# A new order table for a fused RWKV-5 attention and squared-ReLU MLP: engine orders, PSUM banks and filling matmuls

## The chip, the cores and the metric

The kernel runs on one core of a Trainium2 chip. A core has five engines, each of which works off its own queue of instructions in order: TensorE (PE) multiplies matrices into PSUM (eight banks of 128 x 512 float32), VectorE (DVE) and ScalarE (ACT) do elementwise work, GpSimd (POOL) and SyncE (SP) here mainly issue DMAs. The metric is device time in microseconds, median of several executions.

## The reference

Inputs are r, k and v of 4 batches x 8 heads x 768 positions x 48, w and u of 8 x 48, and the MLP's weights of 384 x 2048 and 2048 x 384, all float32.

```python
def _attn_ref(r, k, v, w, u):
    B, H, S, D = r.shape                       # 4, 8, 768, 48
    state = np.zeros((B, H, D, D), dtype=np.float32)
    y = np.zeros_like(r)
    for t in range(S):
        kt, vt, rt = (k[:, :, t].copy(), v[:, :, t].copy(), r[:, :, t].copy())
        cur = np.einsum('bhd,bhe->bhde', u[None] * kt, vt)
        y[:, :, t] = np.einsum('bhd,bhde->bhe', rt, state + cur)
        state = w[None, :, :, None] * state + np.einsum('bhd,bhe->bhde', kt, vt)
    return y

def _moe_ref(x, w_in, w_out):
    h = x @ w_in
    r = np.maximum(h, 0.0)
    g = r * r
    return g @ w_out

# x = attn_out.transpose(0, 2, 1, 3).reshape(3072, 384); out = _moe_ref(x, w_in, w_out)
```

## The kernel before

The 768 positions are cut into six chunks of 128. A unit is one chunk of one batch, so there are 24, numbered chunk by chunk: units 0 to 3 are the first chunk of the four batches. For each unit the attention is computed with matrices of 128 x 128 (positions by positions) for what lies within the chunk, and with a state of 48 x 48 per head for what came before; then the unit's 128 rows go through the MLP.

One unit runs through these steps; the token that stands for each in the table is in brackets, with the engine and the line.

- Load r, k and v (`rt`, `kt` by SP, `vt` by POOL, line 311, or `vtS` by SP, line 309). For units 0 to 5, r and k come in two halves of four heads each (`rt.3.1` is the second half of unit 3's r, line 281) two of them issued by ACT and the others by SP. From unit 6 on (`NH = 6`) one DMA loads two units (line 278).
- Scale r and k by powers of w (`scale.i.0` for r, `scale.i.1` for k; DVE, line 303 for units 0 to 5, line 301 later), into a bf16 tile named rkw. Then both are transposed: in units 0 to 5 by PE (`turn`, line 333) with a copy out of PSUM by ACT (`rkT`, line 337), from unit 6 on by a transposing DMA of SP for two units (`rkD`, line 322).
- For units 0 to 5, k is turned back for the state (`kb`, PE, line 345; `kbT`, ACT, line 349). The product r·k is formed (`rk`, DVE, line 360 or 357).
- Positions by positions (`at`, PE, line 369), masked to the strict lower half on the way out of PSUM (`mask`, DVE, line 377, two halves).
- The diagonal's sums and the state's product (`d` and `s`, PE, lines 389, 398 and 410), the diagonal times v (`dv`, DVE, line 420), the state's update (`sadd`, `sdec`, DVE, lines 424 and 428; bf16 copy `stb`, ACT, line 432). v is cast to bf16 by ACT (`vb`).
- y (`y`, PE, lines 441 and 447), and its copy with dv added (`yb`, DVE, line 456), then its transpose, by PE and ACT (`xturn`, `xT`, lines 477 and 481) or by SP's DMA for two units (`xD`, line 467).
- First matmul of the MLP (`m1.i.q`, PE, line 493: four quarters of one unit, or eight eighths for two units together), `relu` (ACT, line 501), the square (`sqA` on ACT, line 508, or `sqD` on DVE, line 510), second matmul (`m2.i.q`, PE, line 517; the last unit in two halves, line 533), copy out (`osb`, ACT, line 524; lines 543 and 545 for the last unit) and store (`out`, SP, line 553 or 549).

Besides these there are steps that run once: powers of w on ACT and DVE, `ids` and `upper` (POOL builds identities and the mask), `cols`, `copied` and `uwb` (w and u as columns, by PE, DVE and POOL), `end` (ACT: the 128th power of w) and `wend` (POOL, line 268: spread over the state's blocks; it reads what `end` writes), and the weight loads, `I.0` to `I.3` (POOL, line 288, a quarter of the first weight matrix each) and `O.0` to `O.3` (POOL, line 291, of the second). `fill.n` is n matmuls on a constant tile (line 216) whose result nothing reads.

What stands in which order on each engine is written out: `ORDER`, a table of tokens in lines 16 to 80, is walked once from its start to its end, and each token issues its step at the end of its engine's queue. So an engine's order is the order in the table of the tokens that run on it, and the table's relative order between engines has no effect but on the synchronization of buffers. `@` behind a token names the PSUM bank or banks of its output. SP's and POOL's DMAs go into two different queues. The loads of r, k and v rotate through four buffers of two units each.

```python
    for word in ORDER.split():
        what, _, where = word.partition("@")
        name, *a = what.split(".")
        ...
        if where:
            place.update(zip(names(name, *a), (int(x) for x in where)))
        steps[name](*a)
```

Of the kernel before, what the change touches and what calls it, by code (L numbers as in the profile page):

```python
# [16 lines left out]
kt.0.0 kt.0.1 rt.0.0 rt.1.0 I.0 rt.1.1 vt.0 ktA.1.0 lnat.0 fill.26 log@4567 kt.1.1 lnat.1 ids rt.2.0 w.1 upper w.0  # L17
fill.8 cols@1 rt.2.1 wk scale.0.0 kt.2.0 zeros scale.0.1 wr fill.8 turn.0.0@2 kt.2.1 copied uwb turn.0.1@5 rkT.0.0
rt.3.0 rkT.0.1 vt.1 rk.0 fill.10 at.0@63 scale.1.0 rt.3.1 I.3 kb.0@4 mask.0.0 d.0@2 turn.1.0@7 I.2 kbT.0 kt.3.0
mask.0.1 rkT.1.0 vt.2 scale.1.1 vb.0 I.1 kt.3.1 fill.19 turn.1.1@4 dv.0 y.0@3 rkT.1.1 rt.4.0 yb.0 vb.1 rk.1 fill.9  # L20
kb.1@4 kt.4.0 scale.2.0 at.1@31 xturn.0@6 rt.4.1 mask.1.1 d.1@5 turn.2.0@2 xT.0 rkT.2.0 scale.2.1 kt.4.1 fill.5
# [5 lines left out]
kbT.3 m1.2.0@6 scale.4.1 relu.1.1 dv.3 m1.2.1@4 rkT.4.0 sqD.1.3 sqA.0.2 y.3@7 m1.2.2@1 scale.5.0 relu.2.1 sqD.1.1
m1.2.3@2 relu.2.2 sqD.0.1 s.3@5 sqA.1.2 turn.4.1@4 m2.0.0@3 sadd.3 relu.2.3 sadd.2 m2.1.0@1 rkT.4.1 yb.3 relu.2.0
m2.1.1 rk.4 vb.4 scale.5.1 kb.4@7 stb.1 xturn.3@6 at.4@42 kbT.4 m2.0.1 mask.4.1 xT.3 stb.0 s.4@5 mask.4.0 turn.5.0@6
m1.3.0@2 sqD.2.1 rkT.5.0 y.4@0 dv.4 relu.3.0 turn.5.1@6 rt.8 sadd.4 m1.3.3@7 rkT.5.1 yb.4 m2.1.2 sqA.3.0 sqA.2.0  # L30
m2.0.2 kt.8 xturn.4@2 m2.0.3 xT.4 scale.6.0 kb.5@5 osb.0 m2.1.3 scale.7.0 relu.3.3 m1.3.1@2 vtS.6 kbT.5 vb.5
m1.4.0@6 scale.6.1 scale.7.1 at.5@75 relu.4.0 m2.2.0@0 mask.5.0 osb.1 rkD.6 sqA.4.0 m1.4.1@4 sqD.2.3 sqA.2.2 sqD.3.3
m1.4.2@1 relu.3.1 mask.5.1 m2.2.1 stb.3 sdec.4 m1.4.3@6 relu.4.2 rt.10 rk.5 y.5@5 sqA.4.2 scale.8.0 s.5@2 scale.8.1
relu.4.1 m2.2.2 scale.9.0 relu.4.3 vtS.8 m1.3.2@1 sqD.3.1 stb.4 m2.3.0@4 dv.5 relu.3.2 yb.5 m2.2.3 scale.9.1 kt.10
m2.3.1 osb.2 sadd.5 sqA.4.1 m2.4.0@1 sqD.4.3 vb.6 xturn.5@0 sdec.5 at.6@2376 xT.5 rk.6 rkD.8 m2.4.1 stb.2 mask.7.0
stb.5 m1.5.0@0 sqA.3.2 mask.6.0 s.7@7 relu.5.0 mask.7.1 m1.5.3@5 mask.6.1 s.6@2 relu.5.3 m2.4.2 dv.6 out.0 vb.8
y.6@3 dv.7 rt.12 y.7@0 yb.6 m1.5.1@6 yb.7 m2.3.2 sadd.6 relu.5.1 xD.6 scale.10.0 m2.4.3 sqA.5.0 scale.10.1 sqA.5.1
m2.3.3 sadd.7 vtS.10 osb.4 m1.5.2@6 scale.11.1 scale.11.0 m2.5.0@3 relu.5.2 sqD.5.3 kt.12 m2.5.1 sqA.5.2 rk.8
at.8@1520 osb.3 sdec.6 m2.5.2 mask.9.0 rkD.10 m2.5.3 mask.8.0 s.8@4 mask.8.1 osb.5 s.9@2 m1.6.0@7 mask.9.1 m1.6.1@6
sadd.8 relu.6.0 dv.9 kt.14 m1.6.3@5 relu.6.1 dv.8 m1.6.7@1 sqA.6.0 scale.12.0 sadd.9 sqA.6.1 y.9@3 rt.14 y.8@4 vb.10  # L40
m1.6.2@0 yb.8 stb.6 m1.6.5@2 yb.9 relu.6.3 sdec.9 xD.8 m1.6.4@6 relu.6.5 scale.12.1 m2.7.0@3 relu.6.2 sqD.6.3
relu.6.7 vtS.12 m2.6.0@4 scale.13.0 relu.6.4 scale.13.1 m1.6.6@7 sqA.6.2 rk.10 at.10@6120 sqA.6.4 rkD.12 m2.6.1
relu.6.6 mask.10.0 sqA.6.5 s.10@5 sdec.7 m2.7.1 sqA.6.6 sqD.6.7 m2.7.2 stb.7 mask.10.1 stb.9 out.1 m2.7.3 sadd.10
kt.16 mask.11.0 y.10@6 osb.7 m1.8.0@1 dv.10 m1.8.1@2 rt.16 scale.14.0 relu.8.0 sdec.8 m1.8.3@5 relu.8.1 mask.11.1
m2.6.2 stb.8 yb.10 sqA.8.1 s.11@3 y.11@2 relu.8.3 dv.11 m1.8.6@1 vb.12 yb.11 m1.8.4@6 relu.8.6 sadd.11 xD.10 m2.6.3
rk.12 sqA.8.0 relu.8.4 scale.15.0 m1.8.2@2 scale.14.1 m1.8.5@0 relu.8.2 sdec.10 out.4 m2.9.0@7 osb.6 scale.15.1
vtS.14 sqA.8.2 sqD.8.3 m2.8.0@6 relu.8.5 out.3 at.12@4312 sqA.8.6 rkD.14 s.12@0 sqA.8.5 mask.13.0 m2.8.1 sqA.8.4
mask.12.1 m1.8.7@5 mask.12.0 m1.10.1@1 relu.8.7 mask.13.1 out.2 m1.10.3@3 relu.10.1 scale.16.0 vtS.16 s.13@4 sadd.12
y.12@2 dv.12 rt.18 m2.8.2 sdec.11 m1.10.6@5 yb.12 m1.10.5@0 dv.13 relu.10.6 sqD.8.7 y.13@2 stb.10 m2.9.1 relu.10.5
scale.17.0 yb.13 sqA.10.6 m2.8.3 sadd.13 relu.10.3 xD.12 m1.10.2@0 osb.8 sqD.10.3 sqA.10.1 m1.10.0@3 scale.16.1  # L50
kt.18 m1.10.7@1 relu.10.0 scale.17.1 rt.20 at.14@5642 relu.10.2 rk.14 sqA.10.0 m2.9.2 mask.15.1 vb.14 m2.9.3
# [571 lines left out]
```

## Time and profile before

| | us |
|---|---|
| median of 3 runs | 170.97 |
| lowest, highest | 170.62, 171.13 |
| the profiled execution's own time | 171.94 |
| its span | 170.2 |

In the profiled execution the mean granted TensorE clock is 0.988 of full speed. 28.86 MB are moved by DMA, 148 GB/s of reads and writes of device memory over the span. Matmuls of line 493 are 720 with 251 ns each, of line 517 368 with 326 ns each.

How to read the profile: busy time is the time in which an engine executed an instruction, and PEld is the loading of weights into PE, beside its matmuls. In a group's row, `out<-in` names the tiles, `xN` the count, and the bracket behind it the idle time just before the group and what ended it (`<-`). In the chain of waits, and in a list by time, the first two numbers of a row are the start and the length in us. In the DMA queues' rows, the queue's name is followed by packets, megabytes and the time its packets took as a share of all 16 DMA engines. A row with `SPq` or `POOLq` in the list of issues ends with the size and the time from issue to landing. Half a clock of PE is a granted clock of 0.50 in the table by stage.

### The profile page before, as it was taken

What the parts mean: (1) busy time and instruction counts of PE and PEld (TensorE: products, weight loads), DVE (VectorE), ACT (ScalarE), POOL (GpSimd) and SP (SyncE); (2) the same over time, 40 slices, a digit from 0 to 9 for tenths busy, and PEclk for the clock granted to TensorE, in tenths of its full rate; (3) what the DMA queues carried; (4) which work ended last, traced back from release to release, by engine and by line L of the source; (5) the groups of instructions that cost most, each with busy time, mean ns of one, the idle gap of its engine ahead of it and who ended that gap; (6) DMA issues with size and microseconds to landing.
All of it is one profiled execution on the core that took longest, in us unless ns stands there. A gap on an engine that the chain in (4) does not pass through costs nothing.

```text
span 170.2 us, 4733 instructions
## 1 busy us (share of the span) xinstructions
PE 163.9 (96%) x1947; PEld 134.1 (79%) x1947; DVE 122.3 (72%) x243; ACT 129.8 (76%) x255; POOL 15.7 (9%) x36
## 2 busy tenths in 40 slices
PE   7959999999999999999999999999999999999993
PEld 7649999778787697886977887787889789688672
DVE  6567999876999989988988888989697662101100
ACT  3735999888796489698499679688699739599921
POOL 7770670000000000000000000000000000000000
PEclk9996999999999999999999999999999999999999
DMA  3999999999999899999999997998990501100044
GB/s 92 172 279 240 272 194 254 213 201 227 185 181 218 153 214 190 181 212 191 236 182 202 174 251 173 188 288 197 180 232 4 179 6 54 42 0 4 0 164 162
DMA packets 91493, 28.86 MB, mean 170 GB/s; under 512 B 82864, under 2 KB 90672, under 8 KB 91472
## 3 DMA queue, kind: packets, MB, share of 16 engines
q1 hardware_dynamic: 88416, 23.99, 67.5%
q0 software_dynamic: 2624, 4.33, 12.9%
q8 instruction: 15, 0.25, 0.6%
q10 hardware_dynamic: 432, 0.25, 0.6%
q14 instruction: 6, 0.05, 0.1%
HBM read 20.50 MB, written 4.72 MB: 148 GB/s over the span
## 4 chain that ended last, share of the span: by engine, by line
PE 87%; DMA 6%; DVE 3%; SPq 2%; issue 1%; DVEq 0%
PE bank L493 36%; PE bank L517 34%; DMA rt<-in_r_dram 4%; PE bank L369 4%; PE bank L441 3%; DMA xT<-yb 2%; PE bank L398 2%; PE bank L447 2%; SPq L281 2%; PE bank L533 2%; PE bank L333 1%; PE bank L410 1%; PE bank L345 1%; PE bank L216 1%; PE bank L477 1%
## 5 line engine op out<-in xcount | busy, mean ns | idle before, releaser
L493 PE MATMUL bank<-xT,w_in_q 128*128 128x256 bf16 (+1 forms) x720 | 72.6, 251 | 0.1
L501 ACT ACTIVATE gr<-bank 128x512 f32<-128x512 f32 x96 | 55.3, 604 | 19.0 <-PE bank L493 15.2
L517 PE MATMUL bank<-w_out_q,g 128*128 128x384 bf16 x368 | 68.6, 326 | 0.0
L493 PEld LDWEIGHTS <-w_in_q 128*128 128x128 bf16 x720 | 63.8, 113 | 3.9 <-DMA xT<-yb 0.3
L517 PEld LDWEIGHTS <-g 128*128 128x128 bf16 x368 | 34.3, 98 | 18.1 <-issue 0.2
L508 ACT ACTIVATE g<-gr 128x512 bf16<-128x512 f32 x68 | 41.2, 636 | 0.2
L377 DVE TENSOR_TENSOR am<-bank,smask 128x512 bf16<-128x512 f32 x48 | 31.3, 684 | 7.4 <-PE bank L369 6.6
L510 DVE TENSOR_TENSOR g<-gr 128x512 bf16<-128x512 f32 x28 | 19.0, 686 | 17.2 <-ACT gr L501 17.2
L524 ACT COPY osb<-bank 128x384 f32<-128x384 f32 x23 | 11.0, 480 | 5.7 <-PE bank L517 5.6
L456 DVE TENSOR_TENSOR yb<-bank,dv 128x384 bf16<-128x384 f32 x24 | 12.9, 553 | 3.2 <-PE bank L447 2.3
L420 DVE TENSOR_TENSOR dv<-vb,bank 128x384 f32<-128x384 bf16 x24 | 13.0, 548 | 2.2 <-PE bank L410 1.4
L432 ACT CAST stb<-st 128x384 bf16<-128x384 f32 x20 | 10.2, 522 | 0.6 <-DVE st L428 0.6
L301 DVE TENSOR_TENSOR rkw<-rt,wpos 128x384 bf16<-128x384 f32 x18 | 9.8, 551 | 0.8 <-DMA rt<-in_r_dram 0.7
L301 DVE TENSOR_TENSOR rkw<-kt,wneg 128x384 bf16<-128x384 f32 x18 | 9.7, 551 | 0.8 <-DMA kt<-in_k_dram 0.8
L337 ACT COPY rkT<-bank 128x512 bf16<-128x512 bf16 x12 | 7.0, 590 | 3.4 <-PE bank L333 3.4
L216 PE MATMUL bank<-warm 128*128 128x128 bf16 x87 | 8.4, 265 | 1.1 <-DVE warm L161 1.1
L441 PE MATMUL bank<-vb,am 128*128 128x48 bf16 x192 | 8.9, 185 | 0.0
L428 DVE TENSOR_TENSOR st<-st,wend 128x384 f32<-128x384 f32 x16 | 8.8, 550 | 0.0
L424 DVE TENSOR_TENSOR st<-bank,st 128x384 f32<-128x384 f32 x16 | 8.7, 549 | 0.0
L441 PEld LDWEIGHTS <-am 128*128 128x128 bf16 x192 | 7.9, 97 | 0.8
L369 PE MATMUL bank<-rkT 64*128 64x128 bf16 x192 | 8.2, 221 | 0.2 <-ACT rkT L337 0.2
L216 PEld LDWEIGHTS <-warm 128*128 128x128 bf16 x87 | 7.0, 121 | 1.2 <-DVE warm L161 1.0
(75 smaller groups left out, 120.8 us busy)
## 6 DMA issues: line engine op xcount, KB each, us to landing
out_dram<-osb SPq DMA_DIRECT2D x23, 192.0 KB, 2.4
rt<-in_r_dram SPq DMA_DIRECT2D x9, 384.0 KB, 5.8
kt<-in_k_dram SPq DMA_DIRECT2D x9, 384.0 KB, 5.2
vt<-in_v_dram SPq DMA_DIRECT2D x9, 384.0 KB, 4.5
w_in_q<-in_moe_w_in_dram POOLq DMA_DIRECT2D x4, 384.0 KB, 8.3
w_out_q<-in_moe_w_out_dram POOLq DMA_DIRECT2D x4, 384.0 KB, 8.8
vt<-in_v_dram POOLq DMA_DIRECT2D x6, 192.0 KB, 7.3
kt<-in_k_dram SPq DMA_DIRECT2D x11, 96.0 KB, 5.2
```

Source lines behind the costliest of these rows:

```text
L216: nc.tensor.matmul(out=banks[0][:, :128], lhsT=warm, rhs=warm, start=True, stop=True)
L301: nc.vector.tensor_tensor(t["rkw"][:, x, :, :, :D], pair(src), pair(wneg if x else wpos), ALU.mult)
L369: nc.tensor.matmul(out=t["at"][o][:, p, :], lhsT=t["rkT"][sl, 1, p, :], rhs=t["rkT"][sl, 0, p, :], start=True, stop=True,)
L377: nc.vector.tensor_tensor(am, t["at"][o], smask.unsqueeze(1).to_broadcast([C, HP, C]), ALU.mult)
L420: nc.vector.tensor_tensor(t["dv"], t["vb"], t["d"].unsqueeze(2).to_broadcast([C, H, D]), ALU.mult)
L441: nc.tensor.matmul(out=y[:, 2 * p + o, :], lhsT=t[f"am{o}"][:, p, :], rhs=t["vb"][:, 2 * p + o, :], start=(o == 0 and p == 0), stop=c == 0 ...
L456: nc.vector.tensor_tensor(t["yb"], t["y"], t["dv"].rearrange("p h d -> p (h d)"), ALU.add)
L493: nc.tensor.matmul(out=t["h", s][:, a], lhsT=turned, rhs=chunks[c]["xT"][:, b : b + m, n, :], start=(n == 0), stop=(n == NK - 1),)
L501: nc.scalar.activation(t["gr", s], t["h", s], AF.Relu)
L508: nc.scalar.activation(g, x, AF.Square)
L510: nc.vector.tensor_tensor(g, x, x, ALU.mult)
L517: nc.tensor.matmul(out=t["o"], lhsT=chunks[units[i][0]]["g"][:, f, units[i][1], :], rhs=w_out_q[f // 4][:, f % 4, :], start=(f == 0), stop ...
```

## The change

The table of tokens is replaced by another one. Both tables hold the same steps with the same engines; the functions are untouched. Three things differ: the order of the tokens, the bank numbers behind `@`, and the filling matmuls (eight groups of 26, 8, 8, 10, 19, 9, 5 and 2 = 87 before; 26, 20, 10, 9, 3, 13, 1 and 9 = 91 now). Nearly every line of the table is another one; two lines of each, both with `wend`, stand here for them:

```diff
 ORDER = """
...
-scale.3.0 relu.0.3 wend xturn.1@7 rk.2 at.2@26 xT.1 kb.2@0 mask.2.1 sqA.0.0 kt.5.0 d.2@4 turn.3.0@3 vt.3 s.0@7
...
+d.0@1 mask.0.1 end vb.0 kt.3.1 wend scale.1.1 rkT.1.0 fill.13 y.0@3 rt.4.0 dv.0 vt.2 fill.1 turn.1.1@4 yb.0 rt.4.1
...
```

Three places in detail. The first is SP's queue in the opening. Its rows are the loads of halves of r and k; the tiles kt_227 (now kt_217) and rt_206 belong to units 2 and 3, rt_351 and kt_370 (now rt_354 and kt_372) to units 4 and 5. Before:

```order
L281 DMA kt_227<-in_k_dram 128x1x192 x2
L281 DMA rt_206<-in_r_dram 128x1x192 x2
L281 DMA kt_227<-in_k_dram 128x1x192 x2
L281 DMA rt_351<-in_r_dram 128x1x192
L281 DMA kt_370<-in_k_dram 128x1x192
L281 DMA rt_351<-in_r_dram 128x1x192
L281 DMA kt_370<-in_k_dram 128x1x192
```

Now:

```order
L281 DMA kt_217<-in_k_dram 128x1x192 x3
L281 DMA rt_206<-in_r_dram 128x1x192 x2
L281 DMA kt_217<-in_k_dram 128x1x192
L281 DMA rt_354<-in_r_dram 128x1x192 x2
L281 DMA kt_372<-in_k_dram 128x1x192 x2
```

The first half of unit 3's k, which stood behind both halves of its r, now stands ahead of them; and the halves of unit 4 come as r, r, k, k where they alternated.

The second place is POOL's queue in the opening and, behind it, DVE's steps of units 4 and 5. On POOL, vt are loads of v, w_in_q and w_out_q quarters of the two weight matrices, and wend is the copy that waits for ACT's `end`. Before:

```order
L311 DMA vt_162<-in_v_dram 128x8x48
L288 DMA w_in_q3_150<-in_moe_w_in_dram 128x3x512
L288 DMA w_in_q2_149<-in_moe_w_in_dram 128x3x512
L311 DMA vt_310<-in_v_dram 128x8x48
L288 DMA w_in_q1_148<-in_moe_w_in_dram 128x3x512
L268 COPY wend_146<-wend_c_145 64x4x48 x2
L311 DMA vt_310<-in_v_dram 128x8x48
L291 DMA w_out_q0_151<-in_moe_w_out_dram 128x1536
```

Now:

```order
L311 DMA vt_203<-in_v_dram 128x8x48
L288 DMA w_in_q3_150<-in_moe_w_in_dram 128x3x512
L268 COPY wend_146<-wend_c_145 64x4x48 x2
L311 DMA vt_358<-in_v_dram 128x8x48
L288 DMA w_in_q2_149<-in_moe_w_in_dram 128x3x512
L288 DMA w_in_q1_148<-in_moe_w_in_dram 128x3x512
L291 DMA w_out_q0_151<-in_moe_w_out_dram 128x1536
```

`wend` moved ahead of two quarters of the first weight matrix and one load of v, and `O.0`, the first quarter of the second weight matrix, now follows the last quarter of the first one directly. On ACT, `end` moved from unit 1's part of the table to unit 0's.

On DVE, rkw_129 holds scaled r and k of units 4 and 5, am are masks, g squares, st states. From unit 5's scaled r on, before:

```order
L303 TENSOR_TENSOR rkw_129<-rt,wfour 128x8x48
L510 TENSOR_TENSOR g<-gr 128x4x128 x2
L424 TENSOR_TENSOR st_3_140<-bank_256,wend 128x384
L424 TENSOR_TENSOR st_2_139<-bank_76,wend 128x384
L456 TENSOR_TENSOR yb<-bank_258,dv 128x384
L360 TENSOR_TENSOR rk<-rkT 128x512
L303 TENSOR_TENSOR rkw_129<-kt,wfour 128x8x48
L377 TENSOR_TENSOR am_787<-bank_78,smask 128x512
L377 TENSOR_TENSOR am_799<-bank_255,smask 128x512
```

Now:

```order
L303 TENSOR_TENSOR rkw_129<-rt,wfour 128x8x48
L360 TENSOR_TENSOR rk<-rkT 128x512
L510 TENSOR_TENSOR g<-gr 128x4x128 x2
L303 TENSOR_TENSOR rkw_129<-kt,wfour 128x8x48
L377 TENSOR_TENSOR am_784<-bank_76,smask 128x512
L377 TENSOR_TENSOR am_791<-bank_78,smask 128x512
```

Unit 5's scaled k stands ahead of unit 4's masks in both; two updates of the state and a yb that stood between unit 5's r and k stand elsewhere now.

The third place is SP's queue in the middle, from the transposing DMA of units 14 and 15 (rkw3) to that of units 16 and 17 (rkw0). Its other rows are loads of pairs, a transpose of y (xT) and stores. Before:

```order
L322 DMA_TRANSPOSE rkT_1667<-rkw3_130 128x16x128
L553 DMA out_0_dram<-osb_1066 128x384
L309 DMA vt_1715<-in_v_dram 128x16x48
L278 DMA rt_1740<-in_r_dram 128x16x48
L467 DMA_TRANSPOSE xT_1795<-yb_1753 128x6x128
L278 DMA kt_1814<-in_k_dram 128x16x48
L278 DMA rt_1825<-in_r_dram 128x16x48
L322 DMA_TRANSPOSE rkT_1862<-rkw0_127 128x16x128
```

Now:

```order
L322 DMA_TRANSPOSE rkT_1650<-rkw3_130 128x16x128
L553 DMA out_0_dram<-osb_1260 128x384
L309 DMA vt_1712<-in_v_dram 128x16x48
L278 DMA kt_1749<-in_k_dram 128x16x48
L467 DMA_TRANSPOSE xT_1805<-yb_1758 128x6x128
L278 DMA rt_1822<-in_r_dram 128x16x48
L278 DMA rt_1833<-in_r_dram 128x16x48
L553 DMA out_0_dram<-osb_1831 128x384
L278 DMA kt_1878<-in_k_dram 128x16x48
L553 DMA out_0_dram<-osb_1322 128x384
L322 DMA_TRANSPOSE rkT_1912<-rkw0_127 128x16x128
```

One more load and two more stores stand between the two transposes now.

More of the change, by code (lines that the diff above doesn't have):

```diff
@@ L16 @@
 ORDER = """
[L17 to L21, printed above, removed]
@@ L27 @@
[L27 to L31, printed above, removed]
@@ L32 @@
[L32 to L51, printed above, removed]
@@ new lines @@
+turn.5.0@6 sqA.1.2 m2.0.0@1 scale.5.1 stb.0 s.3@7 relu.2.2 mask.4.0 m2.0.1 xT.3 mask.4.1 m2.1.1 vb.4 rkT.5.0 m2.1.2
+s.4@0 y.4@3 dv.4 rt.8 turn.5.1@6 m1.3.0@5 sadd.3 rkT.5.1 yb.4 m2.0.2 relu.3.0 sadd.4 kb.5@6 m2.0.3 sdec.4 vtS.6
+m1.3.3@5 scale.6.0 osb.0 sqA.2.0 scale.7.0 xturn.4@2 m1.3.2@3 kbT.5 kt.8 xT.4 m2.1.3 vb.5 scale.6.1 m1.3.1@6 osb.1
+scale.7.1 stb.3 m2.2.0@0 rk.5 sqA.3.0 rkD.6 sqD.2.1 at.5@74 relu.3.3 m1.4.0@1 mask.5.1 relu.3.1 s.5@5 mask.5.0
+sqA.2.2 m1.4.2@2 relu.4.0 sqD.2.3 m1.4.3@6 stb.1 sqD.3.3 relu.4.2 kt.10 m2.2.1 sadd.5 relu.3.2 m1.4.1@1 sqD.3.1
@@ L80 @@
+m2.23.1@5 osb.22 out.22 osb.23.1 out.23.1
 """
```

88 lines of the change are left out of this document (56 added, 32 removed).

## The prediction, made before the changed kernel was run

> **What bounds the kernel now.** I read the page's busy times first, then a table by stage, then who waits for whom, and last the DMA queues. In the table the columns are the stretch, its length, and for PE, PEld, DVE, ACT and POOL the busy time with its count; then the granted clock, the mean share of the DMA engines and GB/s.
>
> ```profile
> PE 163.9 (96%) x1947; PEld 134.1 (79%) x1947; DVE 122.3 (72%) x243; ACT 129.8 (76%) x255; POOL 15.7 (9%) x36
> ...
> 8.90:12.30 3.40, 1.46 (x23) 1.29 (x23) 2.17 (x5) 1.43 (x3) 2.85 (x4) 1.00 1.11 285
> 12.40:15.80 3.40, 3.40 (x42) 3.01 (x43) 2.27 (x5) 1.07 (x3) 0.00 (x0) 0.50 1.17 218
> 15.82:31.00 15.18, 15.18 (x269) 13.85 (x268) 14.90 (x30) 15.10 (x34) 5.82 (x9) 1.00 1.08 240
> ...
> 60.00:126.00 66.00, 65.94 (x749) 53.63 (x747) 58.24 (x111) 54.26 (x104) 0.00 (x0) 1.00 1.08 206
> ```
>
> From 15.82 us on PE is busy without a gap at full clock; the order cannot shorten that work, since both tables hold the same steps. A new order can gain only ahead of it, and lose anywhere. Two more things are full. DVE and ACT are busy 14.90 and 15.10 us of the 15.18 up to 31 us, and the DMA engines stand at a share of about 1 from 9 to 126 us. So the question for each moved step is which load or DVE step now arrives last.
>
> The opening, in order of time:
>
> ```profile
> 10.13 0.56 DVE L303 TENSOR_TENSOR rkw<-rt,wfour 128x384 bf16<-128x384 f32 x1 [1.63 <-DMA rt<-in_r_dram]
> 10.74 0.40 PE L333 MATMUL bank<-identb,rkw 128*128 128x128 bf16 x4 [1.84 <-DVE rkw L303]
> 12.40 0.61 PE bank L333 x4
> 13.33 0.96 PE bank L216 x9
> 14.29 0.43 PE bank L345 x4
> 14.72 0.54 PE bank L369 x8
> 15.26 0.43 PE bank L477 x3
> 15.78 0.31 PE bank L333 x4
> 16.37 0.66 PE bank L493 x11
> ```
>
> DVE waits 1.63 us for unit 1's r, PE 1.84 us for DVE; then PE works at half clock to 15.8, and m1.0.0 starts at 16.37 (all rows with "PE bank" are from the chain).
>
> **The change, part by part.** *Opening.* Up to turn.1.1 (12.40) the same loads decide, and they stand in the same order. copied now stands ahead of scale.0.1 on DVE, turn.0.1 uses turn.0.0's bank, and there are four more fills (91 for 87): all of it lies ahead of the 10.74 row, under the 1.63 us wait, and I cost it at nothing; without that cover it would be up to the spacing of one DVE step, 0.5 us. Behind 12.40 PE has, ahead of m1.0.0, turn.1.1, nine fills, xturn.0, kb.1, at.1 and turn.2.0: by the rows above 0.61 + 0.96 + 0.43 + 0.43 + 0.54 + 0.31 = 3.28 us, so m1.0.0 at 15.7 where it was at 16.37 (y.0 is done earlier; d.1 and seven fills move behind it or go). That is 0.7 us ahead at half clock, up to twice that if the clock isn't halved. But turn.3.0 stands 2.8 us of PE work later and needs both halves of unit 3's r:
>
> ```profile
> 10.05 0.54 SPq L281 DMA_DIRECT2D rt<-in_r_dram  x1
> rt<-in_r_dram SPq DMA_DIRECT2D x1, 96.0 KB, 7.1
> 10.63 0.68 SPq L281 DMA_DIRECT2D kt<-in_k_dram  x1
> kt<-in_k_dram SPq DMA_DIRECT2D x1, 96.0 KB, 7.5
> ...
> 18.14 0.55 DVE L303 TENSOR_TENSOR rkw<-rt,wfour 128x384 bf16<-128x384 f32 x1
> ...
> 21.20 0.83 PE L493 MATMUL bank<-xT,w_in_q 128*128 128x128 bf16 x12
> 21.87 0.31 PE L441 MATMUL bank<-vb,am 128*128 128x48 bf16 x6
> ```
>
> r's second half was issued at 10.05 and landed 7.1 later, at 17.1. On SP kt.3.0 now goes ahead of both, so r's second half takes the place that kt.3.0 had: 10.63 + 7.5 = 18.1. scale.3.0 can then start at 18.15, as it did before (18.14, there behind DVE's queue): the opening's lead meets this wall. Behind it DVE runs scale.3.0, sadd.1, mask.2.0, scale.3.1 and mask.2.1 for y.2; at 0.47 us from one start to the next (0.60 behind a mask; 10.13 to 10.60 is such a spacing) y.2 can start at 18.15 + 3 x 0.47 + 0.60 + 0.69 + 0.1 = 20.95. Before, y.2 started at 21.87, with m1.1.3 (0.67, from 21.20) ahead of it that now stands behind: 21.20. The gain kept is **0.25 us**.
>
> *POOL's loads.* wend leaves its place in front of vt.3 and the w_out loads, and "end", which it waits for, moves on ACT from between rkT.2.1 and relu.0.3 to behind kbT.0, which belongs to unit 0 and runs under the 1.63 us wait. I take 10 us for wend, and four issues of 0.6 to 1 us behind it: O.0 goes out near 14 us, not at 20.46:
>
> ```profile
> 18.61 0.99 POOL L268 COPY wend<-wend_c 64x192 f32<-64x192 f32 x2 [6.86 <-ACT wend_c L263]
> ...
> 20.46 0.56 POOL L291 DMA_DIRECT2D w_out_q<-in_moe_w_out_dram  x1
> q0 software_dynamic: 387, 0.50, 80.4%
> q1 hardware_dynamic: 375, 0.26, 35.0%
> ...
> q1 hardware_dynamic: 633, 0.43, 96.3%
> q0 software_dynamic: 33, 0.03, 12.6%
> ...
> q0 software_dynamic: 370, 1.04, 95.5%
> q1 hardware_dynamic: 369, 0.07, 11.4%
> ```
>
> These are three windows of the DMA view (packets, MB, share): 15 to 18, 19.8 to 21.2 and 27 to 32 us. q0 is POOL's queue, q1 is SP's. While both have work their packets alternate one to one (387 to 375, 370 to 369). Between 19.8 and 21.2 q0 had run out, and q1 took 633 packets in 1.4 us, 452 a us. In that pause, which POOL's wait made, came most of the loads of units 4 and 5; it goes. With w_out there, a q0 packet takes 0.955 x 5 x 16 / 370 = 0.21 us of an engine and a 768-byte q1 packet 0.35 x 3 x 16 / 375 = 0.045: 64 pairs a us over 16 engines. Units 4 and 5 have eight halves of 96 KB, 128 packets each. From kt.3.1's landing (19.3 by its place) q1 gets some 80 packets until 20 us, then 64 a us: kt.4.1, the fourth half, lands at 20 + (512 - 80)/64 = 26.7; q0's four w_out and three v loads (800 packets) end at 32.5, and kt.5.1 comes at about 32.8. Before:
>
> ```profile
> 19.36 0.54 SPq L281 DMA_DIRECT2D kt<-in_k_dram  x1
> kt<-in_k_dram SPq DMA_DIRECT2D x1, 96.0 KB, 4.4
> ...
> 26.76 0.36 PE L441 MATMUL bank<-vb,am 128*128 128x48 bf16 x8
> ...
> 33.44 0.36 PE L441 MATMUL bank<-vb,am 128*128 128x48 bf16 x8
> ```
>
> kt.5.1 landed at 19.36 + 4.4 = 23.8, and kt.4.1 ahead of it. Who needs them: turn.4.1 now has the same number of steps of each kind ahead of it as y.3 had (26.76), so PE wants it at 26.5 with the gain; scale.4.1 must start at 25.9 and can at 26.7: 0.8 late. scale.5.1 stands ahead of mask.4.0 and mask.4.1 on DVE, so y.4 can start at 32.8 + 0.47 + 0.60 + 0.69 + 0.1 = 34.7; PE wants it at 33.44 less the gain, 33.2 (m2.1.2 is ahead of it in place of m1.3.0): 1.5 late, the 0.8 contained in it. So the loss lies between 0 (landings as before) and 1.5 us. I take **0.9**, above the middle, since the 27 to 32 us window is what will hold there, below the end, since v's packets are shorter than w_out's.
>
> A page of the Trainium skill speaks against this cost: "DMA: Bandwidth & Descriptors", section "Issuing engines are not separate DMA queues", has DMAs of all issuers run on the same 16 engines, so that issuing from several at once saves only the time of issuing. By it an earlier w_out load would shift nothing and this term would be 0, the sum 170.9. Its section on queues and rings has each engine go round its queues packet by packet; the one-to-one counts agree with that.
>
> *SP's stores in the middle.* Between the transposes rkD.14 and rkD.16 stood four loads and one store, now five loads (kt.20 moves ahead) and three stores; one more store stands ahead of rkD.14.
>
> ```profile
> 84.61 0.57 SPq L553 DMA_DIRECT2D out_dram<-osb  x1
> 85.72 2.44 SPq L278 DMA_DIRECT2D rt<-in_r_dram  x1
> 93.43 3.82 SPq L322 DMA_TRANSPOSE rkT<-rkw  x1
> 97.31 0.58 SPq L278 DMA_DIRECT2D kt<-in_k_dram  x1
> 97.99 1.87 SPq L553 DMA_DIRECT2D out_dram<-osb  x1
> rkT<-rkw SPq DMA_TRANSPOSE x1, 6.6
> ...
> 102.66 0.51 PE L369 MATMUL bank<-rkT 64*128 64x128 bf16 x12
> ```
>
> rkD.16 landed at 93.43 + 6.6 = 100.0; at.16 ran at 102.66, 2.6 us later. One load (0.58 to 2.44) and three stores (0.57 to 1.87 each) are 2.3 to 8.1 us; I take 1.5 + 3 x 0.7 = 3.6, near the short ends, because a store costs the long time only right behind a load. The slack is 2.6 plus PE's own delay of 0.65, 3.3: a loss of 0.3 at that value, none to 4.8 at the ends. I count **0.2**.
>
> The other moves of m1, m2, relu, squares and masks stand where DVE is idle 7.8 and ACT 11.7 of the 66 us (60 to 126) and are costed at nothing; what is late next, if that cover is gone, is a bank that relu or mask frees, one DVE step (0.5 to 0.7) each time. The last steps (m2.22.3, m2.23.1, osb, out) keep their order.
>
> Sum: -0.25 + 0.9 + 0.2 = +0.85. The profiled execution took 171.94 us, 0.97 above the median 170.97 of the runs and 1.7 above its span of 170.2; as a difference it carries over: 172.8 against 171.94, **171.8** against the median.
>
> **Rivals.** *Faster: unit 3's r arrives early.* If its second half lands well ahead of 18.1, the opening's lead of 0.7 (half clock) to 1.8 us (the 0.50 of the 12.40 row gone, since PE idles less before 12.3) survives: 169.2 to 170.3, middle 169.9. It decides from a landing at 17.8 on, where more than 0.5 is kept. For it: r's own landing was 17.1. Against: its place behind kt.3.0. *No change:* wend is not early, or q1 is served in time; the pause's loss is 0 and gain and rest cancel: 170.7 to 171.0. *Slower by more: SP.* Stores at 1.1 us each, near the middle of their ends, make 4.8 us against the slack of 3.3: 1.5 late, so 170.97 + 0.65 + 1.5 = 173.1. For it: the 97.99 row; against: the 84.61 row.
>
> **How the numbers follow.** Forecast (0 < loss up to 1.5 and 0.2) 0.45, range 171.2 to 172.4; early r 0.15; no change 0.22; SP 0.18. About 0.3% (0.5 us) is what a measurement tells from no change. Faster: 0.15 and a little of "no change", 0.16. Same: most of "no change" and the forecast's low end, 0.26. Slower 0.58. Leaving out half of "early r" and a third of SP gives 170.2 to 173.0.
>
> **What the next profile would show.** Right: POOL's wend near 10 us without the 6.86 wait; DVE's L303 waits for rt at about 18 and for kt or rt at 26 to 33; PE waits for rkw L303 there, 0.5 to 1.5 us in sum; q0 at over 80% from 19.8 to 21.2. Wrong: scale.3.0 before 17.8, or PE without a wait up to 35 us, or a wait at L369 near 103 us of over 1 us.

## The result, and the profile after

The changed kernel took 173.83 us (median of 4 runs, 172.32 to 174.43) against 171.05 us (170.62 to 171.18): a ratio of 1.0144, 95% interval 1.0104 to 1.0184. It is slower, as forecast, by 2.8 us where 0.85 was forecast, and 0.8 us above the range's end. Run three more times beside the experiments, each time on another chip and beside the kernel before, it took 172.68, 172.41 and 172.18 us, with ratios of 1.0108 (1.0040 to 1.0177), 1.0062 (1.0029 to 1.0095) and 1.0088 (1.0056 to 1.0120). So the change costs some 1%, 1.7 us, and one set of runs differs from the next by more than its own interval says. (All ratios leave out executions more than 1.5% above the fastest of their kernel, which are seven of the twelve in the run without POOL's pause.)

The profiled execution of the changed kernel took 173.64 us, its span 171.9 us. The busy times from its page, then four of PE's waits with what ended them (total, times, longest, in us):

```profile
PE 163.6 (95%) x1951; PEld 133.1 (77%) x1951; DVE 121.7 (71%) x243; ACT 129.6 (75%) x255; POOL 16.2 (9%) x36
```

```profile
PE bank L493 <- DMA w_in_q<-in_moe_w_in_dram: 0.9, 1, 0.9
PE bank L333 <- DVE rkw L303: 0.7, 2, 0.4
PE bank L493 <- DMA xT<-yb: 0.5, 1, 0.5
PE bank L369 <- DMA rkT<-rkw: 0.4, 1, 0.4
```

The table by stage, with the stretches of the prediction:

```profile
8.90:12.30 3.40, 2.75 (x53) 2.35 (x54) 3.04 (x7) 1.80 (x6) 2.67 (x6) 1.00 1.08 274
12.40:15.80 3.40, 3.19 (x62) 2.69 (x60) 3.39 (x7) 2.98 (x7) 3.40 (x6) 1.00 1.14 268
15.82:31.00 15.18, 14.22 (x245) 12.56 (x243) 13.37 (x26) 13.47 (x29) 2.77 (x4) 1.00 1.13 236
60.00:126.00 66.00, 64.84 (x721) 52.37 (x720) 55.20 (x106) 51.72 (x100) 0.00 (x0) 1.00 1.00 194
```

Up to 15.8 us the new order is better: the clock is 1.00 where it was 0.50, and PE is busy 2.75 us of the first 3.40, filling matmuls included, where it was 1.46. m1.0.0 starts at 14.2 instead of 16.3. Behind 15.8 PE, which had next to no gap before, is idle for 0.96 us up to 31 us and for 1.16 us between 60 and 126.

The first loss, by time. POOL's queue, PE's wait, and the landing of unit 3's r (both halves, issued at 9.43 and 10.01):

```profile
10.54 0.72 POOL L268 COPY wend<-wend_c 64x192 f32<-64x192 f32 x2 [0.69 <-ACT wend_c L263]
11.21 0.93 POOL L311 DMA_DIRECT2D vt<-in_v_dram  x1
12.14 1.51 POOL L288 DMA_DIRECT2D w_in_q<-in_moe_w_in_dram  x2
13.64 0.58 POOL L291 DMA_DIRECT2D w_out_q<-in_moe_w_out_dram  x1
```

```profile
19.59 0.86 PE L493 MATMUL bank<-xT,w_in_q 128*128 128x128 bf16 x12 [0.89 <-DMA w_in_q<-in_moe_w_in_dram]
```

```profile
rt<-in_r_dram SPq DMA_DIRECT2D x2, 96.0 KB, 5.7
```

wend is early and O.0 goes out at 13.64, as forecast (10 and 14). But r lands 5.7 us after its issue, at 15.1 and 15.6, not 18.1: the wall that I had set there isn't one. scale.3.0 starts at 16.70, and a start before 17.8 was a sign that the prediction had named for being wrong. (One that it had named for being right came too: q0 is at 81.4% from 19.8 to 21.2 us.) PE runs until m1.0.2, which needs the third quarter of the first weight matrix. That now stands behind unit 2's v on POOL, lands at 19.54 instead of 18.49, and is waited for.

The last loss, in the chain of waits from 96 to 110 us, and DVE's row for the same wait:

```profile
97.34 5.79 DMA rkT<-rkw
...
103.15 0.48 DVE rk L357
...
103.76 0.55 DVE st L428
104.31 0.94 DVE rkw L301 x2
105.25 0.60 DVE am L377
...
106.97 0.36 PE bank L441 x8
```

```profile
103.15 0.69 DVE L357 TENSOR_TENSOR rk<-rkT 128x1024 bf16<-128x1024 bf16 x1 [3.05 <-DMA rkT<-rkw]
```

rkD.16 is issued 3.9 us later than before (97.34 for 93.43) and lands at 103.13. at.16 waits only 0.40 us, but on DVE the same transpose holds rk.16 for 3.05 us at the head of its queue, and with it a state update, three scales and masks; so y.16 (106.97) is late too.

### The profile page after: what moved, and what is told of

The parts are those of the page before. It is cut to its first block, busy times and chain, and to the rows that moved or that the text cites. A ratio compares the mean times of both kernels' runs of the same rounds, so it can differ in the third digit from the quotient of the medians.

```text
span 171.9 us, 4741 instructions
## 1 busy us (share of the span) xinstructions
PE 163.6 (95%) x1951; PEld 133.1 (77%) x1951; DVE 121.7 (71%) x243; ACT 129.6 (75%) x255; POOL 16.2 (9%) x36
## 4 chain that ended last, share of the span: by engine, by line
PE 76%; DMA 14%; DVE 4%; ACT 2%; ACTq 1%; POOL 1%; issue 1%; DVEq 0%
PE bank L493 31%; PE bank L517 31%; DMA rkT<-rkw 7%; DMA w_in_q<-in_moe_w_in_dram 4%; PE bank L369 3%; PE bank L441 2%; DMA xT<-yb 2%; PE bank L447 2%; PE bank L398 2%; PE bank L533 2%; PE bank L333 1%; PE bank L410 1%; DVE rkw L301 1%; ACT L159 1%; DVE am L377 1%; DVE rkw L303 1%
## 5 line engine op out<-in xcount | busy, mean ns | idle before, releaser
L510 DVE TENSOR_TENSOR g<-gr 128x512 bf16<-128x512 f32 x28 | 18.9, 684 | 17.8 <-ACT gr L501 17.8
L357 DVE TENSOR_TENSOR rk<-rkT 128x1024 bf16<-128x1024 bf16 x9 | 6.2, 687 | 7.4 <-DMA rkT<-rkw 7.4
```

Source lines behind the costliest of these rows:

```text
L510: nc.vector.tensor_tensor(g, x, x, ALU.mult)
```

## Experiments

In the diffs only the moved tokens of the table stand. To see where time goes within one execution I take, for a moment of one profile, the sum of PE's steps ahead of it without fills, and the moment at which another profile has done as much; the difference is called PE's lag (below zero: ahead). The reference for it is the second profile of the kernel before.

**The kernel before, again.** No edit.

> The kernel before, unchanged, for a second profile. The first profiled execution of it had half clock on TensorE from 12.4 to 15.8 us and took 171.94 us, 0.9 above the median of the others. Theory A (the half clock belongs to that execution): the second profile shows a granted clock of 1.00 from 12.4 to 15.8, m1.0.0 starts near 15.2 where it started at 16.3, and the time is near 171.0. Theory B (the half clock is in every execution of this order, since PE idles 1.84 us ahead of it): 0.50 is there again, with a time near 171.

Measured: 171.22 us (170.30 to 172.04), ratio 1.0002 (0.9973 to 1.0031), the profiled execution 171.40. Its table by stage:

```profile
8.90:12.30 3.40, 1.81 (x19) 1.81 (x20) 2.42 (x5) 1.41 (x3) 2.83 (x4) 0.76 1.12 290
12.40:15.80 3.40, 3.40 (x55) 3.19 (x54) 2.21 (x6) 1.46 (x4) 0.00 (x0) 0.76 1.19 219
```

Neither theory as it stands. The clock is halved again for 3.4 us, but earlier, from 10.6 to 14.0, so that each of the two stretches shows 0.76. Yet it isn't so in every execution. Of the ten here, five had a mean clock of 0.99 and took 171.40 to 172.04 us, the other five 1.00 and 170.30 to 171.04. Of the 126 executions of the kernel before that stand beside the experiments, 34 had 0.99 or less (median 171.68 us) and 92 had 0.998 or more (170.72); half a clock for 3.4 us of 170 makes a mean of 0.99. Both profiles of the kernel before are of the longer kind. The prediction was summed against an execution that was 0.55 us behind this one: 0.3 by 35 us, the rest near 81 us, where xD.10 had landed 1.1 us later.

**One load forward.** On POOL, I.2 behind I.3.

```diff
-... I.3 ... wend ... vt.2 ... I.2 ... I.1
+... I.3 I.2 ... wend ... vt.2 ... I.1
```

> The changed order with one load moved: the third quarter of the first weight matrix (I.2) stands directly behind I.3 on POOL, ahead of wend and of unit 2's v. It landed at 19.54 us, and m1.0.2 waited 0.89 us for it. Theory A (SP's queue is the wall behind 75 us): the quarter lands near 17.5, the 0.9 us wait goes and PE is 0.9 to 1.3 us further on at 22 us, but the transposed y of units 10 and 11 still lands near 80.4 us and m1.10.1 waits 1.2 to 1.6 us for it instead of 0.49; the time stays within 0.4 us of the changed kernel's 173.8. Theory B (waits add up): the time falls by 0.9 to 1.3 us, to about 172.7.

Measured: 173.15 us (171.64 to 174.36), ratio 1.0111 (1.0066 to 1.0156). The quarter landed at 19.24, not 17.5, and m1.0.2 no longer waited for it; but unit 2's v landed at 20.06 instead of 16.56, ACT's vb.2 with kbT.2 behind it came late, and PE waited 0.76 us at y.2 and 0.51 us at m1.1.3. In this run as in the changed kernel POOL's queue brings only so many of these bytes by 20 us; the order chooses which of them is late. The time lies between the two theories, and the ratio is near the 1.0101 that the changed kernel's own four runs have in the mean. rkD.16 landed at 102.07 without a wait: SP's queue was quicker in this execution, with the same order.

**rkD.16 back ahead of the stores.**

```diff
-... out.8 kt.20 out.5 rkD.16
+... rkD.16 out.8 kt.20 out.5
```

> The changed order with the transpose of units 16 and 17 (rkD.16) ahead of the two stores and one load (out.8, kt.20, out.5) that stand ahead of it on SP, as it was before. It is issued near 93.8 instead of 97.34 us and lands near 100 instead of 103.13. Theory A: the 0.40 us wait of at.16 goes, DVE's rk.16 no longer holds the state updates and scales behind it, y.16 is not late, and the time falls by 0.6 to 0.8 us to about 173.1. Theory B (the load and stores that now come behind it make the next one late, m1.14.7 for xD.14 with its 0.04 us of slack, or rkD.18): the time stays within 0.3 us of 173.8.

Measured: 172.00 us (170.78 to 173.59), ratio 1.0048 (1.0017 to 1.0079). SP's row and the DMA's:

```profile
92.44 3.51 SPq L322 DMA_TRANSPOSE rkT<-rkw  x1
```

```profile
rkT<-rkw SPq DMA_TRANSPOSE x1, 6.5
```

Landed at 98.93, 3.45 us ahead of at.16; PE's lag is 0.26 at 35 us and 0.25 at 106. Against the first run's 173.83 us the gain is more than the forecast 0.7; against the mean ratio of the changed kernel's four runs, 1.0101, it is about 0.9 us, and most of that lies at the end of the kernel (below). Over all runs of the changed order, the ratios with rkD.16 in its changed place go from 1.0062 to 1.0177 (eight, mean 1.0118), those with rkD.16 forward from 1.0022 to 1.0117 (six, mean 1.0053). Without the two that have one more instruction (below) the first mean is 1.0098; what is left, 0.0045 or 0.8 us, is little more than the end of the kernel makes.

**Both transposes forward.** As before, and xD.10 ahead of rt.16 and vtS.14.

```diff
-rt.16 ... vtS.14 ... xD.10
+xD.10 rt.16 vtS.14
```

> As the run before, and also the transpose of y of units 10 and 11 (xD.10) ahead of the load of unit 16's r and unit 14's v. It is issued near 73.9 instead of 76.38 us and lands near 78.5 instead of 80.41. Theory A: the 0.49 us wait of m1.10.1 goes too and the lead of 0.8 us that the opening has left is kept to the end: 172.3 to 172.7. Theory B (something else, the loads that now land later or DVE, is late in its place between 80 and 105 us): 173.1 or more, with a new wait in that stretch.

Measured: 173.05 us (172.37 to 173.63), ratio 1.0117 (1.0084 to 1.0150): theory B, though not by its place alone. xD.10 landed 3.3 us ahead of m1.10.1, but v of unit 14 was late, held ACT 1.2 us, and m1.10.6 waited 0.56 us; and in this profile the opening had lost more, m1.0.2 having waited 1.68 us.

**The changed kernel again, three times.** No edit.

> The changed kernel, unchanged, for a second profile and on the chip of the three runs behind it. Three profiles with the same opening (the changed kernel and the two runs with rkD.16 moved) had PE 0.70 us ahead, 0.26 us ahead and 0.45 us behind the kernel before at 22 us. Theory A (the third quarter of the first weight matrix ends the wait of m1.0.2 in every execution, but lands anywhere from 19.5 to 20.7 us): m1.0.2 waits 0.5 to 1.7 us for it here too, and the rest of the loss comes again between 100 and 108 us, at the transpose rkD.16, if that lands behind 102.5. Theory B (the profile was a chance): no wait for that quarter, none for rkD.16, and a time near 172.

> The changed kernel once more, unchanged, on the chip of the three others, for its spread and a third profile. Both theories: 172.7 to 173.8, from about 172.2 to 174.8. Theory P expects kt.5.1 at 26 us or later in the profile; theory Q a wait at a transpose behind 60 us.

> The changed kernel unchanged, on the chip of the two others. Both theories: 172.4 to 173.8; the last two stores 2.6 to 2.9 and 2.1 to 2.3 us.

Measured: the times above. The four profiles, PE's lag in us behind the second profile of the kernel before:

| | 1st | 2nd | 3rd | 4th | mean | forecast |
|---|---|---|---|---|---|---|
| at 28 us (opening) | -0.51 | 0.72 | -0.68 | 0.39 | -0.02 | -0.25 |
| added 28 to 35 us (loads of units 4, 5) | 0.00 | 0.00 | 1.20 | 0.00 | 0.30 | 0.9 |
| added 35 to 115 us (SP's transposes) | 1.94 | 0.05 | 1.01 | 0.05 | 0.76 | 0.2 |
| last store's longer time | 0.75 | 0.77 | 0.58 | 0.67 | 0.69 | 0 |
| time less 171.40 | 2.24 | 1.61 | 2.16 | 1.17 | 1.80 | 0.85 |

The reference is an execution with half a clock in its opening. Against one without, the opening is worse than the table has it, by an estimated 0.5 us: that is how far ahead of the reference the run with 24 fills and a full clock is (below).

In all four m1.0.2 waits for the third quarter (0.89, 0.62, 0.24, 0.96 us). In the second m1.0.0 waited 1.11 us besides, since ACT's xT.0 stands behind vb.1, and unit 1's v had landed at 14.40 instead of 13.22:

```profile
14.42 0.51 ACT L318 CAST vb<-vt 128x384 bf16<-128x384 f32 x1 [1.50 <-DMA vt<-in_v_dram]
```

The third profile is the prediction's case. SP's issue of unit 5's k with its time to landing, DVE's row, and PE's waits:

```profile
17.67 1.25 SPq L281 DMA_DIRECT2D kt<-in_k_dram  x2
```

```profile
kt<-in_k_dram SPq DMA_DIRECT2D x1, 96.0 KB, 13.6
```

```profile
31.92 0.56 DVE L303 TENSOR_TENSOR rkw<-kt,wfour 128x384 bf16<-128x384 f32 x1 [1.65 <-DMA kt<-in_k_dram]
```

```profile
PE bank L410 <- DVE am L377: 0.7, 1, 0.7
PE bank L369 <- DMA rkT<-rkw: 0.6, 1, 0.6
```

kt.5.1, the second of the pair, landed at 31.89 (forecast 32.8, before 23.8), scale.5.1 waited 1.65 us for it and PE 0.7 us for the masks behind. In the first two profiles it was issued two us earlier and landed at 27.1 and 26.2; in the fourth it landed at 31.67, but PE was late itself.

**The kernel before without POOL's pause.** Only `end` moves, so that wend doesn't wait.

```diff
-... yb.1 end rt.5.1 ... relu.0.3 wend ...
+... kbT.0 end ... I.1 wend ...
```

> The kernel before with one step moved: end stands behind kbT.0 on ACT, so POOL's wend finds it done and the loads behind it on POOL, the three v and four w_out, go out from about 12.5 us instead of 19.6; POOL's order and all else stay. This takes away the pause of POOL's queue that the prediction's 0.9 us rests on. Theory of the prediction: kt.4.1 and kt.5.1 land near 27 and 33 us instead of 22 and 23.5, scale.5.1 and y.4 come 1 to 1.5 us late, and the time rises by 0.9 (0 to 1.5) to about 171.8. Theory A (the loads of units 4 and 5 have room): they land later, kt.5.1 at 26 to 29, but ahead of scale.5.1 (30.4), and the time stays within 0.3 us of the kernel before.

Measured: 173.56 us (170.95 to 177.71) against 170.95, ratio 1.0057 (1.0010 to 1.0105). POOL's queue, the DMA queues from 19.8 to 21.2 us, DVE's two waits from 25 to 36 us (the first as a total, the second as the row) and PE's longest there:

```profile
12.03 0.72 POOL L268 COPY wend<-wend_c 64x192 f32<-64x192 f32 x2
...
13.61 0.56 POOL L291 DMA_DIRECT2D w_out_q<-in_moe_w_out_dram  x1
```

```profile
q0 software_dynamic: 136, 0.28, 82.6%
q1 hardware_dynamic: 134, 0.09, 25.4%
```

```profile
DVE rkw L303 <- DMA rt<-in_r_dram: 2.0, 1, 2.0
```

```profile
32.03 0.56 DVE L303 TENSOR_TENSOR rkw<-kt,wfour 128x384 bf16<-128x384 f32 x1 [0.79 <-DMA kt<-in_k_dram]
```

```profile
PE bank L345 <- DVE yb L456: 1.2, 1, 1.2
```

In the same 1.4 us q1 took 134 packets instead of 633 (561 in the second profile). The second half of unit 5's r landed at 27.7 us instead of 22.3, kt.5.1 at 32.0 instead of 23.2, and PE went from 1.25 us ahead at 28 us to 0.77 behind at 35: 2.0 us. This is the prediction's mechanism, in the kernel before, at more than its price, but mostly by another load than it named. DVE waited 2.0 us for r, yb.3 stands behind that on DVE and freed its bank late, and this is PE's 1.2 us at 31, ahead of kt.5.1's landing; for the masks behind kt.5.1 PE waited only 0.2 us. The Trainium skill ("DMA: Bandwidth & Descriptors", section "Issuing engines are not separate DMA queues") has issuing from several engines at once save only the time of issuing, since all DMAs run on the same 16 engines and interleave; the trace agrees that both queues share the engines, and shows what follows from it: when POOL issues decides whose bytes wait. So the section does not speak against this term, and it was wrong to work out a 0 from it.

**POOL's old queue in the changed kernel, then its pause.** First (with rkD.16 forward) POOL's order as before and vb.2 behind kbT.2; then also the pause, by `end` behind relu.0.3 and sadd.1 behind mask.2.0.

```diff
-ids ... vt.0 ... I.3 ... end ... wend ... vt.2 ... I.2 ... I.1 ... O.0 ... vt.3
+vt.0 ids ... I.3 I.2 vt.2 I.1 ... end wend ... vt.3 O.0
```

```diff
-... kbT.0 end wend ... sadd.1 ... mask.2.0
+... relu.0.3 end wend vt.3 O.0 ... mask.2.0 sadd.1
```

> The changed order with rkD.16 moved (172.0 us as it was run before), and POOL's queue in the order of the kernel before: v of unit 0 ahead of the identities, then I.3, I.2, v of unit 2, I.1, wend, and v ahead of each w_out quarter; on ACT vb.2 stands behind kbT.2, since v of unit 2 lands 2 us later. end keeps its early place, so there is no pause in POOL's queue. Theory A (POOL's order decides when the third quarter lands, and that decides the opening): I.2 lands near 18.1, m1.0.2 waits 0.3 us at most, PE is 1.0 to 1.5 us ahead of the kernel before at 22 to 26 us, and then loses most of it where unit 5's k lands last (near 31 us, as in the run without POOL's pause): 171.0 to 171.8. Theory B (the lead is lost anyway by 22 us): 172.0 within 0.3.

> The run with POOL's old queue (172.6 us, from 170.68 to 174.43), with the pause of POOL's queue put back: end stands behind relu.0.3 on ACT, so that wend, and the loads of v and w_out behind it, go out near 17 us instead of 12.6, and sadd.1, which reads wend, behind mask.2.0 on DVE. Nothing else differs. Theory P (without the pause the loads of units 4 and 5 land so late, kt.5.1 at 30.5 in the profile, that they stop DVE in many executions): kt.5.1 lands at 22 to 26, the median falls by 1.2 us or more to 171.4 or less, and the spread shrinks from 3.7 to under 2 us. Theory Q (the spread has another source, in SP's queue behind 60 us): median 172.2 or more, spread over 2.5.

Measured: 172.60 us (170.68 to 174.43), ratio 1.0060 (1.0021 to 1.0100); with the pause 171.57 (170.82 to 172.86), ratio 1.0024 (0.9995 to 1.0053). The first one's profiled execution was its fastest: the quarter landed at 18.13, nothing waited for it, and kt.5.1 landed at 30.51; DVE waited 1.03 us for that, and PE not at all behind it. The median is above both theories. That it mostly takes longer fits kt.5.1 landing later; no profile of such an execution was taken. With the pause kt.5.1 landed at 23.53 and the spread fell from 3.75 to 2.04 us, both just short of theory P. The intervals overlap, so the median's gain isn't shown by these two runs alone.

**The pause alone, and with rkD.16 forward.**

```diff
-... end ... wend ... vt.2 ... I.2 ... I.1 ... O.0 ... sadd.1
+... vt.2 ... I.2 ... I.1 ... end wend O.0 ... mask.2.0 sadd.1
```

> The changed kernel with that pause alone: wend stands behind I.1 instead of ahead of unit 2's v on POOL, and waits for end behind relu.0.3; sadd.1 behind mask.2.0. The other order of POOL, of SP and of all else is the changed one. Theory P: kt.5.1 lands at 22 to 26 us instead of 26 to 27, the scale of it never waits, and the time falls by 0.5 to 1.2 us below the changed kernel's; what stays is the wait for the third quarter of the first weight matrix and rkD.16: 171.8 to 172.6. Theory Q: no gain, 172.7 or more.

> As the run before, and rkD.16 ahead of out.8, kt.20 and out.5 on SP. Theory P, with the two losses apart from one another: a further 0.4 to 0.8 us below the run before, 171.2 to 172.0. Theory Q (SP's queue is the whole loss): as the run with rkD.16 moved alone, 172.0, whatever POOL does.

Measured: 172.32 us (171.60 to 173.83), ratio 1.0077 (1.0043 to 1.0112), and 171.40 (170.49 to 172.58), ratio 1.0022 (0.9991 to 1.0053); the changed kernel beside them 172.41, 1.0062. The pause alone gains nothing in the median, though kt.5.1 lands at 23.46; with rkD.16 forward what is left can't be told from the kernel before.

**m1.1.3 for m1.0.2.** rkD.16 forward, these two on PE in each other's place, out.19 early.

```diff
-m1.0.2@1 ... relu.0.2 ... m1.1.3@3 ... relu.1.3
+m1.1.3@1 ... relu.1.3 ... m1.0.2@3 ... relu.0.2
```

> The changed order with rkD.16 ahead of out.8, kt.20, out.5 as in the run before, with m1.1.3 (whose quarter of the weights has landed by 15.5 us) and m1.0.2 (whose quarter lands at 19.5 to 20.7) in each other's place on PE, their banks left in place, and out.19 directly behind osb.19. Theory A (m1.0.2 came too early for its load): PE does m1.1.3, turn.3.1 and y.2 first, 1.2 us of work, the 0.85 us wait falls to 0.3 or less, and the time falls by 0.5 to 0.8 us below the 172.0 of the run with rkD.16 moved alone. Theory B (the whole opening is bound by the bytes of POOL's queue): m1.1.1, which needs the last quarter (landed at 22.5 to 24.5), waits in its place, and nothing is gained: 172.0 within 0.3.

Measured: 171.53 us (171.16 to 173.60), ratio 1.0044 (1.0006 to 1.0083). m1.0.2 starts as its quarter lands (20.30), without a wait, and m1.1.1 waits 0.74 us for the last quarter (23.29): theory B's place. The median is 0.5 below the 172.0, but the ratios, each against the kernel before beside it, are 1.0044 and 1.0048: no gain is shown.

**The gap of the kernel before.** First 24 fills in it; then 14 fills, mask.0.0 ahead of scale.1.0 and fewer later fills; then also xD.10 ahead of rt.16 and out.3 behind rkD.14.

```diff
-... d.0@2 turn.1.0@7 ...
+... d.0@2 fill.24 turn.1.0@7 ...
```

```diff
-scale.1.0 ... mask.0.0 d.0@2 turn.1.0@7 ... fill.19 ... fill.9 ... fill.5 ... fill.2
+mask.0.0 scale.1.0 ... d.0@2 fill.14 turn.1.0@7 ... fill.9 ... fill.8
```

> The kernel before with 24 more filling matmuls ahead of turn.1.0, in the 1.6 to 1.8 us in which PE waits for unit 1's r and after which its granted clock was 0.50 and 0.76 in the two profiles of this order (it was 1.00 in all profiles of the changed order, where PE idles less there). Theory A (the idle stretch lowers the clock): the clock is 1.00 from 8.9 to 15.8 us, m1.0.0 starts at 15.0 to 15.4 instead of 15.87 and 16.26, and the time falls by 0.4 to 0.9 us to about 170.2, unless a load stops the lead behind it. Theory B (the clock has another cause): it is below 1.00 again, and the time stays within 0.3 us of the kernel before.

> The kernel before with the first mask of unit 0 ahead of unit 1's first scale on DVE (it has its input 0.8 us before that scale has its load), 14 filling matmuls in PE's gap ahead of turn.1.0, and the later fills of the opening cut from 19, 9, 5, 2 to 9, 8, 0, 0. POOL's pause stays. Theory A (behind 10 us the opening is bound by DVE): scale.1.1 starts 0.5 us earlier, m1.0.0 starts near 14.3 instead of 15.3 to 15.9, PE has no wait behind it as long as the loads come as in the last profiles, and the time falls by 0.5 to 1.0 us to about 170.2, below both kernels. Theory B (I.2, landed at 18.0, or SP's transposes stop it): no gain, 170.9 within 0.3, with a wait of m1.0.2 or one of L369 or L493 behind 60 us.

> As the run before, and on SP xD.10 ahead of the load of unit 16's r, and the store out.3 behind rkD.14 instead of ahead of it: the two transposes that had 0.05 and 0.2 us of slack in the first profile of the kernel before, with slow DMAs, and 1.7 and 2.6 in the latest one. Theory A: nothing where DMAs are quick, up to 0.5 us less where they are slow, so the median is the same or 0.2 lower than that of the run before and the highest times come down. Theory B: the load or the store is late in their place, as in the run with both transposes first: 0.3 or more above the run before.

Measured: 170.89 us (170.09 to 171.75), ratio 0.9990 (0.9959 to 1.0021); 170.75 (169.97 to 172.12), 0.9994 (0.9964 to 1.0023); 170.75 (170.30 to 171.38), 0.9989 (0.9963 to 1.0015). With the fills the clock holds:

```profile
8.90:12.30 3.40, 3.40 (x60) 3.20 (x59) 2.14 (x5) 1.15 (x3) 2.85 (x4) 1.00 1.08 269
12.40:15.80 3.40, 3.35 (x64) 2.90 (x62) 3.04 (x8) 2.33 (x6) 0.00 (x0) 1.00 1.19 214
```

In the profiles PE is 0.49, 0.96 and 0.75 us further on; in the medians nothing is gained. The lead is one over a reference with half a clock: that execution took 171.40 us, 0.45 above the median of the kernel before beside the first of these runs (170.95), and the one with 24 fills took 170.92, like its own median. None of the 36 executions of the three has a mean clock below 0.998. So the fills do away with the executions that have half a clock, a quarter of all in the kernel before, and leave the median where it was. The two moved transposes gain nothing in the median either; the highest time fell from 172.12 to 171.38. No version here is measurably faster than the kernel before.

**The end of the kernel.** In the first profile of the changed kernel the last store took 2.3 us, in both of the kernel before 1.5. Over the profiles: 2.1 to 2.3 us in all six of the changed order with rkD.16 in its new place, 1.5 in all six with rkD.16 forward and in all six of the old order. The DMA view shows an 8 KB packet of q14 beside the late ones. The two differ also by one waiting instruction on ACT. So one ACT instruction was added to the changed kernel, and to the one with the pause:

```diff
+        pad=lambda: nc.scalar.copy(spare, up),
...
-osb.16 ...
+osb.16 pad ...
```

> The changed kernel with one ScalarE instruction more (a copy of one column to a tile that nothing reads, behind osb.16, where ACT has idle time). In all five profiles with the changed order of rkD.16, an 8 KB packet of the instruction queue q14 ran 0.2 to 0.8 us behind the issue of the last store, and the last two stores took 2.6 to 2.9 and 2.1 to 2.3 us; in all six with rkD.16 moved it ran 1.5 us ahead of that issue, and they took 1.8 and 1.5. The second six have one waiting instruction more on ACT. Theory F (the packet is ACT's next block of instructions, and its place hangs on the count of ACT's instructions): with one more it runs 1.5 us ahead, the stores take 1.8 and 1.5, and the time falls by 0.6 us below the changed kernel run beside it. Theory G (the late rkD.16 itself causes it): 2.6 and 2.1 again, no gain.

> The run with POOL's pause restored (172.3) with the same ScalarE instruction more; rkD.16 stays late. The run with rkD.16 moved as well took 171.4. Theory F: 0.6 us of that 0.9 was the tail, and this one takes 171.7. Theory G: 172.3 as without the instruction, since all of it was the wait for rkD.16.

The changed kernel beside them (167.6 to 168.9 us; last store issued at 167.62), then the one with the added instruction, 167.5 to 168.2 us, and from 168.6 us on (last store issued at 168.84):

```profile
q14 instruction: 1, 0.01, 3.8%
...
out_dram<-osb SPq DMA_DIRECT2D x1, 64.0 KB, 2.2
```

```profile
q14 instruction: 1, 0.01, 2.8%
...
out_dram<-osb SPq DMA_DIRECT2D x1, 64.0 KB, 1.5
```

The packet moved from behind the last store's issue to ahead of it (167.88 and 167.64), and the store took 1.5 us; the run with the pause shows the same (1.5). So theory F holds for its place: one ACT instruction decides it. That the packet itself holds up the store is argued from the timing. The forecast time does not hold: 173.71 us (173.14 to 174.74), ratio 1.0174 (1.0136 to 1.0212), and 173.75 (172.99 to 175.01), ratio 1.0177 (1.0133 to 1.0220), against 172.18 of the changed kernel. In their profiles PE's lag at 28 us is 0.40 and 0.57, as in the one beside them (0.39). What they lost more lies at SP's transposes again, 1.3 and 1.2 us from 70 to 110 us, and 0.5 at 33 us in the second; the waits of the first (its lines stand one lower in the file):

```profile
PE bank L494 <- DMA xT<-yb: 0.4, 1, 0.4
PE bank L370 <- DMA rkT<-rkw: 0.2, 1, 0.2
```

xD.10 landed at 81.1 and 81.9 us there, and at 79.7 in the one beside them. Why SP's queue is later in these two is open. One instruction whose result nothing reads moved the median by 1.5 us, nearly as much as the whole change; so a median that moves so far after one edit doesn't by itself show that the moved step was the cause.

## Why the prediction was right and wrong

- **Direction and bound: right.** The order can't shorten PE's work, and every loss of PE's shows as a load or transpose that lands last; only the loss at the last store is of another kind.
- **The opening gain of 0.25: its wall was wrong.** r's second half was put at the landing that k had had (18.1); it landed at 15.6. The true wall was four PE steps further on: m1.0.2 and the third quarter of w_in, which I had noticed only as one of "four issues". I moved wend past I.2 and v but did not price I.2's own delay, 1.05 us. The gain kept, -0.02 in the mean of four profiles, is near the 0.25 by accident, and it is a lead over an execution with half a clock. The sum was made against such an execution (171.94 us) and carried over to a median of executions that mostly have none; 0.96 us lies between the two kinds, and none of the changed kernel's four profiles has half a clock in its opening.
- **POOL's pause, 0.9 (0 to 1.5): mechanism right, size not constant.** It costs 2.0 us in the profile of the kernel before without the pause, mostly by unit 5's r, which the prediction did not price, and 1.2 in the third profile of the changed one, with kt.5.1 at 32 us as worked out; it costs nothing where SP issues that load two us earlier, or where PE is late at y.4 already. I priced one landing and no spread.
- **SP's stores, 0.2 (0 to 4.8): the mis-sized term.** The delay of the issue was 3.9 us, taken as 3.6; that they agree is luck, since out.8 and out.5 stand right behind loads and took 1.23 and 1.66 us, not 0.7, and the extra load 0.43, not 1.5. The sum counted 0.2 where its own figures give 0.3. What failed is the slack, 2.6 + 0.65: I credited PE with a delay of my own other terms, where PE was 0.1 us late, and took the landing from one execution, while rkD.16 landed from 101.8 to 103.2 us in the four profiles of the changed kernel. And I named who waits on PE, not what is queued behind rk.16 on DVE, where that step now stands ahead of three scales that it followed, a move costed at nothing. It cost 0.76 in the mean, up to 0.8 at rkD.16 alone in the first profile; the rest there is xD.10, which had 0.05 us of slack before and so took back any lead. The rival "slower by more: SP", 173.1, came nearest.
- **The last steps "keep their order": wrong.** m2.22.2 and out.19 moved, among others; no run tests them alone. But the end cost 0.69 us in the mean of the profiles, a term put at nothing, beside an instruction packet that no row of the order shows.
- **The range** rested on terms that were each taken once. Two of them vary by 1 to 2 us between executions of one kernel, and both walls can be met in one execution: the third profile has 1.2 and 1.0.

## What to carry to other kernels

Where an order is changed, list every load and transpose by slack (landing to first use) before pricing anything, those with none first: they are where a gain ends. Price a moved DMA by what its queue's bytes ahead of it need, and ask on each engine what stands behind the instruction that waits for it. Where DMA engines are full, take landings from several profiles before putting a term at zero, look at the clock of all executions before one of them is taken as the reference, and repeat the whole comparison before trusting 1%.
